# Linear attention and a gated MLP in one order: the first half of the written order is new, and the f, k and q loads span 112 rows

## The chip, the cores and the metric

The kernel runs on one core of a Trainium2 chip. The metric is the device time of one execution in microseconds (us).

## What is computed

For 4 batches, 8 heads, 768 tokens and 48 channels a head, a linear attention with a decaying state; its output, 4 x 768 x 384, goes through a gated MLP with a spatial product over tokens.

```python
f = 1 / (1 + exp(-f_logit))
for t in range(768):
    state = f[t, :, None] * state + outer(k[t], v[t])     # per batch and head, 48 x 48
    y[t] = q[t] @ state
h = maximum(x @ w_in, 0)                                  # x: y of all heads, 384 wide; h: 1024 wide
u, v = h[..., :512], h[..., 512:]
v_n = (v - mean(v)) / sqrt(var(v) + 1e-6)
v_s = einsum('ts,bsd->btd', w_spatial, v_n) + b_spatial[:, None]
out = (u * v_s) @ w_out
```

## The kernel before

The attention goes in 24 chunks n of 128 tokens, six for each batch. Two heads share the 128 partitions: the channels of one on rows 0 to 47, of the other on rows 64 to 111. Rows 48 to 63 and 112 to 127 of the host array `fkq` are padding.

The whole program is one list, `PLAN`: each word is a step, a letter name and its numbers, and the steps are issued in the order of the list. Every engine, and the queue of SyncE (SP) that issues all loads, so works through its own part of the list strictly in that order; a step that waits holds up all that stand behind it on its engine. `BESIDES` names the steps that go to GpSimd (POOL) instead of their usual engine.

The steps of a chunk n:

- `LF:n` loads f, into row block 0 of one of three tiles `fkq`. For n below 6 (`SUMMED`) it loads 128 tokens x 384 from `fn` (192 KB), and `LK:n` loads k and q apart (512 KB). From 6 on, `LF:n` loads f, k and q in one (768 KB). `LQ:n` loads v (192 KB) into one of two tiles.
- `c:n` clamps f (L322), `e:n` takes exp and ln of it on ScalarE (ACT; L326, L327). `z:n` makes running sums: for n below 6 on TensorE (PE) by a product with a triangle (L337), later as a scan on VectorE (DVE; L332). `h:n` and `g:n` exponentiate the sums (ACT; L343, L348), `k:n` and `q:n` multiply them into k and q (DVE; L354, L358).
- `X:n` makes the products of q and k (PE, L382), `m:n` masks them (DVE, L392), `w:n` copies another part (ACT, L388). `YS:n` (L434), `kv:n` (L406) and `Yq:n` (L446) are products for the output and the state; `r0`, `r1`, `r2` (DVE; L412 to L425) carry the state on; `ys:n`, `xt:n`, `xh:n`, `xl:n` copy, transpose and split the output. `fm:n` notes the last decay of the chunk (POOL).

The MLP's weights come in six pieces of 768 KB (`LV`, `LU`, `LO`, L243) and go through `ca`, `ct`, `ch`, `cl` to a high and a low part. V and U pieces share two buffers `words`: a buffer is free when `ch` and `cl` of its piece are through, and the next of these loads waits for that. `w_spatial` comes in pieces of 384 KB (`LW`, L284), split by `wh` (ACT or POOL) and `wl` (DVE, L294). `V:b,u` (L491), `U:b,th,c` (L576), `S:b,th,c` (L590) and `O:b,th,tt` (L621) are the MLP's products; `vr`, `bs`, `na`, `nb`, `nc`, `vn`, `vh`, `vl` normalize v, `sg`, `sm`, `sh`, `sl` gate. V and U of a batch's half need its three chunks; S needs all six vn of its batch.

`D:count` issues products of zeros (L674) into a bank that nothing reads. A load of f, k and q may go out only when the steps that read its tile's old content are through: `LF:6` after `X:3`, `LF:7` after `X:4`.

Of the kernel before, what the change touches and what calls it, by code (L numbers as in the profile page):

```python
# [825 lines left out]
```

## Time and profile before

| | |
|---|---|
| median of 3 runs | 356.96 us (356.3 to 357.31) |
| the profiled execution | 356.21 us |
| its span, first to last instruction | 354.4 us |
| mean granted clock of TensorE | 0.979 |
| busy: PE, weight loads (PEld) | 338.0 us (95%), 313.5 us (88%) |
| busy: DVE, ACT, POOL | 211.9 us (60%), 172.5 us (49%), 77.6 us (22%) |
| moved by DMA | 36.15 MB, mean 102 GB/s |

Busy is the time in which an instruction of the engine ran. Products are pipelined, so a busy TensorE isn't one at its peak. The granted clock is a share of full speed (2.4 GHz); 0.5 is 1.2 GHz. An average over the span says little here, since the first 60 us and the rest have different limits; the rows below are by stretch.

### The profile page before, as it was taken

The numbers are of one execution on the slowest core, as the hardware profiler recorded it, in microseconds if no ns is written. First come the engines' busy times: TensorE is split into PE (matmuls) and PEld (weight loads), VectorE is DVE, ScalarE is ACT, GpSimd is POOL, SyncE is SP. The second block draws the span as 40 slices with busy tenths as digits, with TensorE's granted clock in tenths as the row PEclk, the third lists the DMA queues.
The fourth block names the chain that finished last, engine by engine and source line by source line (L and its number), as shares of the span: only waits on it lengthen the run. The fifth ranks groups of instructions, "written<-read, shape, count | busy, mean of one in ns | idle before, by whom it ended". The sixth has DMA issues, their size and how long they took to land.

```text
span 354.4 us, 10435 instructions
## 1 busy us (share of the span) xinstructions
PE 338.0 (95%) x4565; PEld 313.5 (88%) x4565; DVE 211.9 (60%) x407; ACT 172.5 (49%) x355; POOL 77.6 (22%) x94
## 2 busy tenths in 40 slices
...
GB/s 229 288 264 332 276 193 212 35 191 64 162 190 127 93 130 49 107 143 74 39 138 0 158 1 92 91 24 2 44 46 2 2 44 3 22 68 0 0 68 77
DMA packets 14838, 36.15 MB, mean 102 GB/s; under 512 B 1472, under 2 KB 10048, under 8 KB 14784
## 3 DMA queue, kind: packets, MB, share of 16 engines
...
q14 instruction: 16, 0.13, 0.1%
HBM read 30.67 MB, written 4.72 MB: 100 GB/s over the span
## 4 chain that ended last, share of the span: by engine, by line
PE 84%; DVE 5%; DMA 5%; ACT 1%; SPq 1%; issue 1%; POOL 1%; DVEq 0%; ACTq 0%; POOLq 0%
PE mm L590 29%; PE mm L621 14%; PE mm L576 13%; PE mm L491 12%; PE bp L382 6%; DMA fkq<-fkq 5%; PE bp L434 3%; PE bp L446 3%; PE bp L406 2%; PE mm L458 2%; DVE q L358 1%; DVE fkq L354 1%; POOL fkq L322 1%; PE mm L337 1%; DVE w_spl L294 0%
## 5 line engine op out<-in xcount | busy, mean ns | idle before, releaser
L606 POOL TENSOR_TENSOR uT<-gt,uT 128x384 f32<-128x384 f32 x32 | 34.5, 1087 | 151.8 <-DVE gt L599 64.0
L599 DVE TENSOR_TENSOR gt<-mm,b_bc 128x384 f32<-128x384 f32 x32 | 17.7, 553 | 48.3 <-PE mm L590 48.2
L590 PE MATMUL mm<-w_sph,vnh 128*128 128x384 f32 x192 | 39.4, 340 | 0.0
L590 PE MATMUL mm<-w_sph,vnl 128*128 128x384 f32 x192 | 39.0, 338 | 0.0
L590 PE MATMUL mm<-w_spl,vnh 128*128 128x384 f32 x192 | 38.9, 338 | 0.0
L581 ACT ACTIVATE uT<-mm 128x384 f32<-128x384 f32 x32 | 15.5, 488 | 45.1 <-PE mm L576 41.1
L590 PEld LDWEIGHTS mm<-w_spl,vnh 128*128 128x128 f32 x192 | 34.2, 188 | 0.0
L590 PEld LDWEIGHTS mm<-w_sph,vnl 128*128 128x128 f32 x192 | 34.2, 188 | 0.0
L590 PEld LDWEIGHTS mm<-w_sph,vnh 128*128 128x128 f32 x192 | 33.8, 188 | 0.3
L322 POOL TENSOR_SCALAR fkq<-fkq 112x512 f32<-112x512 f32 (+1 forms) x14 | 23.7, 1692 | 45.6 <-DMA fkq<-fkq 26.4
L382 PE MATMUL bp<-q,fkq 48*64 48x112 f32 x768 | 24.8, 271 | 4.6 <-DVE q L358 4.1
L382 PEld LDWEIGHTS bp<-q,fkq 48*64 48x64 f32 x768 | 20.2, 141 | 6.6 <-DVE q L358 4.6
L614 DVE TENSOR_TENSOR gl<-uT,gh 128x384 fp32r<-128x384 f32 x32 | 17.5, 563 | 13.8 <-ACT gh L610 13.8
L610 ACT CAST gh<-uT 128x384 fp32r<-128x384 f32 x32 | 16.0, 511 | 19.6 <-POOL uT L606 18.8
L354 DVE SCALAR_TENSOR_TENSOR fkq<-fkq 112x512 f32<-112x512 f32 x24 | 17.8, 742 | 10.9 <-ACT fkq L348 5.6
L567 DVE TENSOR_TENSOR vnl<-vr,vnh 128x512 fp32r<-128x512 f32 x21 | 14.8, 716 | 15.6 <-ACT vnh L557 15.6
L332 DVE TENSOR_TENSOR_SCAN fkq<-runs,fkq 112x512 f32<-112x512 f32 x18 | 23.2, 1296 | 0.2 <-ACT fkq L327 0.2
L576 PE MATMUL mm<-xTh,w_inh 128*128 128x384 f32 x96 | 23.0, 348 | 0.0
L505 ACT ACTIVATE vr<-mm 128x512 f32<-128x512 f32 x24 | 14.3, 598 | 18.0 <-PE mm L491 17.6
L491 PE MATMUL mm<-w_inh,xTh 128*128 128x512 f32 x72 | 22.3, 417 | 0.0
L576 PE MATMUL mm<-xTh,w_inl 128*128 128x384 f32 x96 | 22.1, 338 | 0.0
L621 PE MATMUL mm<-w_outh,gh 128*128 128x384 f32 x96 | 22.1, 346 | 0.0
...
## 6 DMA issues: line engine op xcount, KB each, us to landing
fkq<-fkq SPq DMA_DIRECT2D x18, 768.0 KB, 5.2
val<-vv SPq DMA_DIRECT2D x24, 192.0 KB, 4.3
out<-osb SPq DMA_DIRECT2D x23, 192.0 KB, 2.0
words<-w_cv SPq DMA_DIRECT2D x4, 768.0 KB, 8.3
fkq<-fkq SPq DMA_DIRECT2D x6, 512.0 KB, 5.9
late<-w_cv SPq DMA_DIRECT2D x2, 768.0 KB, 5.7
fkq<-fn SPq DMA_DIRECT2D x6, 192.0 KB, 3.0
...
```

The source lines that it names most:

```text
L322: other("c", n, nc.vector).tensor_scalar(f, f, -LOGIT_MOST, None, op0=ALU.max)
L332: return nc.vector.tensor_tensor_scan(f[0:DP], runs, f[0:DP], 0.0, op0=ALU.mult, op1=ALU.add)
L354: other("k", n, nc.vector).scalar_tensor_tensor(k, f, 1.0 / F_LEAST, k, op0=ALU.min, op1=ALU.mult)
L382: nc.tensor.matmul(sc[to, e, cs], k[dr, at:at + C], qs[n % 2][dr, j, chunk], start=True, stop=True)
L491: nc.tensor.matmul(acc, xs[:, c, ut * P:(ut + 1) * P], ws[:, c, G:FF], start=i == 0, stop=i == 3 * KX - 1)
L576: nc.tensor.matmul(acc[:, 0:TH], ws[:, kx, cs], xs[:, kx, :], start=i == 0, stop=i == 3 * KX - 1)
L590: nc.tensor.matmul(acc[:, 0:TH], vns.of((b, ks))[va][:, cs], w_sp_s[wb][:, ks, th * TH:(th + 1) * TH], start=i == 0, stop=i == 3 * KS - 1,)
L599: nc.vector.tensor_tensor(gts.take((b, th, c)), mm.of(("s", b, th, c))[:, 0:TH], b_bc[:, th * TH:(th + 1) * TH], op=ALU.add)
L606: nc.gpsimd.tensor_tensor(uT, gts.of((b, th, c)), uT, op=ALU.mult)
L610: nc.scalar.copy(gs.take((b, th, c), HU)[0], uTs.of((b, th, c)))
L614: nc.vector.tensor_tensor(lo, uTs.of((b, th, c)), hi.bitcast(F32), op=ALU.subtract)
L621: nc.tensor.matmul(acc[:, 0:DM], gs.of((b, th, c))[ga][:, ts], w_out_s[wb][:, c, :], start=c == cs[0] == 0 and ga == wb == 0, stop=c == cs ...
```

## The change

Three things change.

1. The first half of `PLAN` is written anew, up to the step `xt:11`; from there to the end it is word for word the old one. Products of zeros: 11, 5 and 3 before (19), now 4, 5, 3 and 4 (16).
2. `BESIDES`, up to chunk 13: q:5, q:6, q:7, q:8, q:11, q:13, the casts wh:1,0 and wh:0,1, and vn:0,4, vn:0,5, vn:1,1, vn:1,2 now go to POOL, r2:1 and r2:4 too, c:4 and c:15 as well. c:3, c:5, c:6, c:7 and r2:0, r2:8, r2:12 go back to DVE.
3. The host array has 112 rows in place of 128 for each pair of heads, and the loads of f, k and q span 112 partitions: 672 KB in place of 768, 448 in place of 512. The compute steps read rows 0 to 111, as before.

```diff
-    constants LF:0 LF:1 units:1 W0 c:1 c:0 e:0 units:0 D:11 LF:2 c:2 e:1 z:0 LQ:1 LV:0 g:0 z:1 LK:0 h:0 k:0 q:0 LK:1 g:1
+    W0 LF:0 constants c:0 units:0 LF:1 c:1 e:0 LK:0 LK:1 D:4 e:1 z:0 LV:0 LQ:0 g:0 h:0 k:0 units:1 z:1 g:1 runs h:1 q:0
...
-    c:1 c:3 r2:0 c:5 r2:2 c:6 r2:3 c:7 c:9 c:8 r2:6 c:10 r2:7 r2:8 c:13 r2:10 r2:12 c:16 c:17 r2:14 c:19 r2:16 c:20
-    r2:18 c:22 r2:22
+    c:1 c:4 wh:1,0 r2:1 r2:2 r2:3 q:5 r2:4 wh:0,1 q:6 c:8 q:7 r2:6 c:9 q:8 vn:0,4 vn:0,5 c:10 r2:7 q:11 c:13 r2:10
+    vn:1,1 q:13 vn:1,2 c:15 c:16 c:17 r2:14 c:19 r2:16 c:20 r2:18 c:22 r2:22
...
-            nc.sync.dma_start(ins[n % 3], fkq[b, u])
+            nc.sync.dma_start(ins[n % 3][0:DP], fkq[b, u])
...
-        nc.sync.dma_start(ins[n % 3][:, 1:3], fkq[b, u, :, 1:3])
+        nc.sync.dma_start(ins[n % 3][0:DP, 1:3], fkq[b, u, :, 1:3])
...
-        y = np.full((B, NU, P, J * T), pad, np.float32)
+        y = np.full((B, NU, DP, J * T), pad, np.float32)
```

What the new list does to the queues shows in the order of each engine's instructions. A row names the line (all lines of the changed kernel are one higher), the operation, and the tile it writes and reads; the number behind a tile's name tells its buffers apart (`fkq_112`, `_113`, `_114` hold chunks 0, 1, 2, then 3, 4, 5).

The head of SP's queue before: LF:0 to LF:2, LQ:1, LV:0 (words_157), LK:0, LK:1, LQ:0, LV:1 (words_158), LF:3.

```order
L308 DMA fkq_112<-fn 128x384
L308 DMA fkq_113<-fn 128x384
L308 DMA fkq_114<-fn 128x384
L318 DMA val_116<-vv 128x384
L243 DMA words_157<-w_cv 128x2x768
L314 DMA fkq_112<-fkq 128x1024
L314 DMA fkq_113<-fkq 128x1024
L318 DMA val_115<-vv 128x384
L243 DMA words_158<-w_cv 128x2x768
L308 DMA fkq_112<-fn 128x384
```

And now: LF:0, LF:1, LK:0, LK:1, LV:0, LQ:0, LQ:1, LF:3, LF:2, LV:1.

```order
L309 DMA fkq_112<-fn 128x384
L309 DMA fkq_113<-fn 128x384
L315 DMA fkq_112<-fkq 112x1024
L315 DMA fkq_113<-fkq 112x1024
L244 DMA words_157<-w_cv 128x2x768
L319 DMA val_115<-vv 128x384
L319 DMA val_116<-vv 128x384
L309 DMA fkq_112<-fn 128x384
L309 DMA fkq_114<-fn 128x384
L244 DMA words_158<-w_cv 128x2x768
```

LK:0 has moved from the sixth place to the third, and LF:2 from the third to the ninth, behind LF:3, which needs k:0.

The same queue further on, before: LU:1 (words_157), LW:0,1, LQ:4, LF:6, LK:5, LU:0 (words_158), LF:7.

```order
L243 DMA words_157<-w_cv 128x2x768
L284 DMA late_161<-w_spT 128x2x384
L318 DMA val_115<-vv 128x384
L310 DMA fkq_112<-fkq 128x1536
L314 DMA fkq_114<-fkq 128x1024
L243 DMA words_158<-w_cv 128x2x768
L310 DMA fkq_113<-fkq 128x1536
```

And now: LU:1 (words_158), LQ:4, LU:0 (words_157), LF:6, LQ:5, LK:5, LW:0,1, LF:7.

```order
L244 DMA words_158<-w_cv 128x2x768
L319 DMA val_115<-vv 128x384
L244 DMA words_157<-w_cv 128x2x768
L311 DMA fkq_112<-fkq 112x1536
L319 DMA val_116<-vv 128x384
L315 DMA fkq_114<-fkq 112x1024
L285 DMA late_161<-w_spT 128x2x384
L311 DMA fkq_113<-fkq 112x1536
```

LU:0 now stands ahead of LF:6 and LK:5.

DVE's queue around the sixth chunk, before: k:5, z:6, q:5, xl:2, r0:4, r1:4, two wl, r2:4, m:5, cl:U,1, q:6; k:6 is next.

```order
L354 SCALAR_TENSOR_TENSOR fkq_114<-fkq_114 112x512
L332 SCALAR_TENSOR_TENSOR fkq_112<-runs,fkq_112 112x512
L358 TENSOR_TENSOR q_124<-fkq_114,F_122 112x8x64
L473 TENSOR_TENSOR xTl_137<-mm_131,xTh_136 128x3x128
L414 TENSOR_TENSOR sB_127<-bp_135,sA_125 112x192
L420 TENSOR_TENSOR sA_126<-bp_135,sB_127 112x192
L294 TENSOR_TENSOR w_spl<-spat_160,w_sph 128x2x384
L294 TENSOR_TENSOR w_spl<-late_161,w_sph 128x2x384
L425 TENSOR_TENSOR sA_126<-sA_126,F_121 112x192
L392 TENSOR_TENSOR sc_118<-bp_134,mask 128x512
L272 TENSOR_TENSOR w_inl<-words_157,w_inh 128x3x256
L358 TENSOR_TENSOR q_123<-fkq_112,F_121 112x8x64
```

And now: c:6, xl:2, ct:U,1 (three), r0:4, r1:4, k:5, z:6, c:7, wl:2,0, cl:U,1; m:5 and k:6 are next.

```order
L323 TENSOR_SCALAR fkq_112<-fkq_112 112x512
L474 TENSOR_TENSOR xTl_137<-mm_131,xTh_136 128x3x128
L258 TENSOR_SCALAR words_158<-words_158 128x768
L259 SCALAR_TENSOR_TENSOR words_158<-words_158 128x768
L260 SCALAR_TENSOR_TENSOR words_158<-words_158 128x768
L415 TENSOR_TENSOR sB_127<-bp_134,sA_125 112x192
L421 TENSOR_TENSOR sA_126<-bp_134,sB_127 112x192
L355 SCALAR_TENSOR_TENSOR fkq_114<-fkq_114 112x512
L333 SCALAR_TENSOR_TENSOR fkq_112<-runs,fkq_112 112x512
L323 TENSOR_SCALAR fkq_113<-fkq_113 112x512
L295 TENSOR_TENSOR w_spl<-spat_160,w_sph 128x2x384
L273 TENSOR_TENSOR w_inl<-words_158,w_inh 128x3x256
```

The q steps and r2:4 have left this queue, and c:6 and c:7, which wait for LF:6 and LF:7, have come into it.

## Rows read from the trace of the kernel before

**Rows 1.** Busy time by long stretches: the stretch and its length in us, busy us and count of each engine, the granted TensorE clock, the DMA engines' share and GB/s.

```profile
0.00:60.00 60.00, 51.17 (x1090) 41.64 (x1091) 46.64 (x82) 46.42 (x92) 19.59 (x29) 0.91 0.75 253
60.00:120.00 60.00, 60.00 (x1006) 55.86 (x1005) 51.65 (x97) 36.13 (x73) 13.75 (x18) 1.00 0.41 139
120.00:344.00 224.00, 223.88 (x2456) 213.39 (x2455) 113.14 (x229) 88.70 (x188) 44.30 (x47) 1.00 0.16 53
```

**Rows 2.** The same by stretches of 4 us, from 12 to 48; the engines stand in the order PE, PEld, DVE, ACT, POOL.

```profile
12.00:16.00 4.00, 3.56 (x80) 3.33 (x84) 3.24 (x6) 0.94 (x2) 0.63 (x1) 0.50 0.72 201
16.00:20.00 4.00, 4.00 (x126) 3.67 (x120) 3.90 (x8) 2.67 (x7) 1.56 (x3) 0.70 0.80 276
20.00:24.00 4.00, 3.06 (x86) 2.29 (x84) 3.50 (x7) 2.31 (x6) 0.19 (x1) 1.00 0.68 208
24.00:28.00 4.00, 3.63 (x51) 2.85 (x51) 3.59 (x6) 3.33 (x7) 0.00 (x0) 0.65 0.99 308
28.00:32.00 4.00, 3.66 (x146) 3.23 (x144) 2.94 (x7) 2.46 (x6) 2.69 (x4) 0.92 0.99 359
32.00:36.00 4.00, 3.52 (x85) 2.81 (x89) 3.84 (x7) 3.19 (x7) 1.15 (x1) 1.00 0.92 327
36.00:40.00 4.00, 4.00 (x76) 3.00 (x68) 3.59 (x5) 2.57 (x6) 2.78 (x3) 1.00 1.01 364
40.00:44.00 4.00, 3.25 (x133) 2.85 (x133) 3.97 (x7) 4.00 (x10) 1.20 (x1) 1.00 0.52 204
44.00:48.00 4.00, 3.63 (x76) 2.64 (x74) 4.00 (x7) 3.88 (x9) 2.80 (x2) 1.00 0.46 147
```

**Rows 3.** The chain of waits over the first 70 us: start, length in us, what. A DMA's length runs from its issue to its landing. L382 is X, L491 V, L576 U.

```profile
3.15 7.84 DMA fkq<-fkq
...
11.09 0.69 DVE fkq L354
...
12.44 3.27 PE bp L382 x64
...
17.78 4.88 DMA fkq<-fkq
...
23.36 0.35 DVE sA L425
...
24.37 1.04 PE bp L382 x32
...
30.19 5.98 DMA fkq<-fkq
...
47.36 0.61 DVE fkq L354
...
48.01 1.00 PE bp L382 x32
49.01 0.48 PE bp L446 x30
...
49.49 2.29 PE mm L491 x9
...
63.17 1.79 PE mm L576 x9
```

**Rows 4.** DMA issues of the page: out<-in, queue, count, KB each, median us from issue to landing.

```profile
fkq<-fkq SPq DMA_DIRECT2D x18, 768.0 KB, 5.2
val<-vv SPq DMA_DIRECT2D x24, 192.0 KB, 4.3
words<-w_cv SPq DMA_DIRECT2D x4, 768.0 KB, 8.3
fkq<-fkq SPq DMA_DIRECT2D x6, 512.0 KB, 5.9
fkq<-fn SPq DMA_DIRECT2D x6, 192.0 KB, 3.0
```

**Rows 5.** ACT in order of time: start us, us, line, operation, tiles. g:0 and h:0.

```profile
6.78 0.60 ACT L348 ACTIVATE fkq<-mm 112x512 f32<-112x512 f32 x1
7.27 0.59 ACT L343 ACTIVATE F<-mm 112x512 f32<-112x512 f32 x1
```

**Rows 6.** DVE in order of time, as above: the second cl:V, and r2:4. The last row is from the view of the tile fkq: the clamps on DVE with the least, median and greatest ns.

```profile
29.69 0.95 DVE L272 TENSOR_TENSOR w_inl<-words,w_inh 128x768 fp32r<-128x768 f32 x1
...
44.52 0.76 DVE L425 TENSOR_TENSOR sA<-sA,F 112x192 f32<-112x192 f32 x1
...
L322 DVE TENSOR_SCALAR fkq<-fkq x10: 353/416/828, 3.2 to 229.7; 112x512 f32<-112x512 f32 x7, 128x384 f32<-128x384 f32 x3
```

**Rows 7.** PE in order of time: the first and second group of zeros, and two products that came after a stop (idle us and its releaser in brackets).

```profile
2.11 2.53 PE L674 MATMUL mm<-junk 128*128 128x256 bf16 x11 [2.11 <-DVE rescale L212]
...
8.41 0.72 PE L674 MATMUL mm<-junk 128*128 128x256 bf16 x5
...
22.46 0.26 PE L446 MATMUL bp<-sA,q 48*64 48x48 f32 x2 [0.57 <-POOL ends L367]
...
24.37 1.04 PE L382 MATMUL bp<-q,fkq 48*64 48x112 f32 x32 [0.74 <-DVE q L358]
```

**Rows 8.** POOL: its two-input product by shape, from the groups by line (busy us and mean ns of one, then idle before), and its clamps from the view of the tile fkq.

```profile
L606 POOL TENSOR_TENSOR uT<-gt,uT 128x384 f32<-128x384 f32 x32 | 34.5, 1087 | 151.8 <-DVE gt L599 64.0 <-ACT uT L581 62.8 <-ACT fkq L348 20.7
...
L322 POOL TENSOR_SCALAR fkq<-fkq x14: 1163/1488/3148, 3.9 to 209.9; 112x512 f32<-112x512 f32 x11, 128x384 f32<-128x384 f32 x3
```

More of the change, by code (lines that the diff above doesn't have):

```diff
@@ new lines @@
+    e:13 r1:10 r2:10 LQ:12 LF:14 sh:0,0,2 na:1,0 nb:1,0 sg:0,1,3 sm:0,0,0 h:12 g:12 xt:9 S:0,1,1 sh:0,0,3 nc:1,0
+    sg:0,1,0 c:14 z:13 q:12 sl:0,0,3 ca:O,0 YS:11 ur:0,1,0 k:12 kv:11 ys:10 X:12 LF:15 r0:11 r1:11 Yq:11 vn:1,1 e:14
+    h:13 g:13 xt:10 xh:10 sg:0,1,1 z:14 LQ:13 xh:9 k:13 xl:9 ys:11 m:12 sm:0,1,3 fm:12 q:13 S:0,1,2 YS:12 w:12 xl:10
+    kv:12 X:13 sg:0,1,2 vh:1,1 r0:12 sh:0,0,0 Yq:12 U:0,1,2 vn:1,2 c:15 ct:O,0 r1:12 sh:0,1,3 w:13 LF:16 r2:12 xt:11
+    xh:11 xl:11 ys:12 sl:0,0,0 V:1,3 U:1,0,2 ur:0,1,2 vn:1,0 vh:1,0 vl:1,0 h:14 q:14 V:1,5 vl:1,1 m:13 sl:0,1,3 vr:1,5
@@ new lines @@
+    k:16 e:17 vh:1,5 q:16 z:17 sh:0,1,1 LF:18 V:2,1 w:15 YS:15 kv:15 X:16 ur:1,0,0 vr:2,1 w:16 xh:14 r0:15 bs:2,1 Yq:15
+    vl:1,5 xl:14 m:16 c:18 sl:0,1,0 sl:0,1,1 LQ:17 r1:15 fm:15 r2:15 U:1,0,1 ur:1,0,1 h:17 LF:19 ys:15 S:1,0,0 q:17 c:19
+    e:19 sg:1,0,0 S:1,0,2 S:1,1,1 od:0,0,2 g:17 V:2,2 k:17 sg:1,0,2 YS:16 kv:16 sm:1,0,2 od:0,0,1 r0:16 X:17 Yq:16
+    vr:2,2 LQ:18 r1:16 r2:16 sm:1,0,0 O:0,1,0 sg:1,1,1 fm:16 fm:17 ur:1,0,3 S:1,0,1 z:19 sg:1,0,1 sh:1,0,0 e:18 xt:15
+    z:18 bs:2,0 O:0,1,2 bs:2,2 m:17 h:18 S:1,1,2 sl:1,0,0 w:17 g:18 ys:16 q:18 oc:0,1,0 k:18 YS:17 kv:17 r0:17 X:18
@@ new lines @@
+    sg:2,0,1 ur:2,0,1 sm:2,0,1 S:2,0,3 xt:20 h:22 sl:1,1,0 w:21 U:2,0,2 oc:1,0,0 q:22 g:22 k:22 ur:2,0,2 sm:2,0,2 LQ:22
+    LQ:21 YS:21 sg:2,0,3 kv:21 sl:1,1,3 bs:3,1 r0:21 X:22 Yq:21 r1:21 O:1,1,2 S:2,1,0 U:2,1,3 od:1,0,2 sg:2,1,0 ur:2,1,3
+    r2:21 S:2,0,0 sg:2,0,0 sm:2,0,0 sh:2,0,2 S:2,1,3 sl:2,0,2 xh:20 xl:20 e:23 oc:1,1,2 z:23 O:1,1,0 h:23 g:23 V:3,2
+    sg:2,1,3 od:1,0,1 vr:3,2 bs:3,2 od:1,0,0 O:1,1,1 ys:21 xt:21 oc:1,1,1 U:2,0,3 ur:2,0,3 sm:2,0,3 sh:2,0,1 q:23
+    oc:1,1,0 na:3,0 nb:3,0 k:23 od:1,1,2 sm:2,1,3 S:2,1,2 S:2,1,1 LQ:23 sg:2,1,2 sh:2,0,3 nc:3,0 fm:22 fm:23 U:2,1,1
```

106 lines of the change are left out of this document (46 added, 60 removed).

## The prediction, made before the changed kernel ran

> **What bounds the kernel now.** I read busy time in long stretches first. TensorE is busy for 51.17 of the first 60 us, for all of the next 60, and for 223.88 of the 224 us after that [rows 1]. So from 60 us on the kernel goes at the rate of its products, and only the first 60 us have anything to give: 8.83 us without a product, and a mean granted clock of 0.91. The stretches of 4 us show that nearly all of this lies ahead of 48 us: VectorE (DVE) is busy for 32.57 of the 36 us from 12 to 48, the 16 DMA engines are near full from 24 to 40, and the granted clock is 0.50 to 0.70 from 12 to 20 and 0.65 from 24 to 28 [rows 2]. The chain of waits names what holds the early products [rows 3]: the first k and q of step X:0 land at 10.99 us (3.15 + 7.84), DVE's k:0 starts at 11.09 and X:0 at 12.44; LK:2 lands at 22.66 and X:2 starts at 24.37; LF:6 lands at 36.17, its clamp, exponent, running sum, k:6 and q:6 follow, and X:6 starts at 48.01. Loads decide, and behind each of them the DVE queue.
>
> **The mark.** X:6 is a good mark because both orders put the same products ahead of it: z:0 to z:5, X, YS and kv of chunks 0 to 5, Yq:0 to Yq:4, xt:0 to xt:4 and V:0,0 to V:0,2. Only the products of zeros differ (19, now 16). From step xt:11 on both lists are one. If TensorE stays full behind X:6, as it does before, the time moves by as much as X:6 does.
>
> **The start.** LK:0 had 1,536 KB in front of it in the SP queue, now 384 (sizes in [rows 4]). From LK:0 at 10.99 to LF:6 at 36.17 the queue brought 7,232 KB (the loads of its order by their sizes), 287 KB a us [rows 3, 4]. LK:0 with 448 KB of its own would be complete 1,216 KB sooner: 4.2 us, at 6.7. Then its factor is late next: g:0 ends at 7.38 and h:0 at 7.86 on ScalarE (ACT) [rows 5], and with units:1 moved behind h:0 nothing delays them. k:0 at about 7.5: **3.5 us earlier**.
>
> **Work on DVE between k:0 and k:6.** q:5 and q:6 go to GpSimd (POOL): 2 x 0.61. One half of the w_spatial remainders (L294) now stands behind k:6: 0.87. The state decays r2:1 (0.35) and r2:4 (0.76) go to POOL, r2:0 comes at the 0.35 of r2:1: 0.76 less. In come the clamps c:3, c:5 and c:2, which stood ahead of k:0 (0.36 each), and c:6, c:7 (0.42 each); c:4 leaves: 1.56 more [rows 6]. Sum: 1.22 + 0.87 + 0.76 - 1.56 = **1.3 us less**; I take 1.0, as the steps overlap a little. On ACT two weight casts of 0.8 us leave for POOL, which has slack (0.00 to 2.80 busy in 4 us) [rows 2].
>
> **New waits in the DVE queue.** Before, DVE stood 3.4 us of the 36 (36 - 32.57). With the work pulled forward it meets loads that aren't there. c:3 waits for LF:3, which SP may issue only after k:0 and which stands behind 2,432 KB: complete at 13.0 by the rate above, 1 to 1.5 us of wait. k:2 waits for LK:2, 4,224 KB in: 10.99 + (4,224 - 2,048)/287 = 18.6, about 1 us. The long one is c:6. DVE would reach it at about 33: it has 39 instructions from k:0 to there, at 32.57 us for the 60 from 12 to 48 [rows 2] 21.2 us, with 2.5 of waits so far and some 1.5 at the start for g:1 and X; LF:6 stands 9,248 KB in, at 36.1; and if the queue moves as in the full stretch from 24 to 40 (340 GB/s, the mean of its four rows [rows 2], 332 KB a us), at some 34.5, since LU:1 ahead of it can't go out before cl:V,1 has freed its buffer at about 27. That is 2 to 3 us with xl:2, ct:U,1, r0:4, r1:4, k:5 and z:6 queued behind. Together 4.0 to 6.0 us of waiting in place of 3.4: **0.6 to 2.6 us back**.
>
> **The sum.** k:6 ended at 47.97 [rows 3]. 47.97 - 3.5 - 1.0 + (0.6 to 2.6) = 44.1 to 46.1. X:6 then has YS:5 and kv:5 in front of it, which wait for m:5: 0.3 to 0.4 more, 44.4 to 46.5. Middle 45.4, **2.6 us ahead of 48.01**. The profiled execution took 356.21 us (span 354.4 and 1.8 around it), so it would take 353.6; it lies 0.75 below the median of the runs shown, 356.96, from which the forecast is **354.4 us**.
>
> **Edits costed at nothing.** The products of zeros take 0.14 to 0.23 us each (0.72/5, 2.53/11 [rows 7]) and lie where TensorE waits for loads; without that cover the 16 would cost 3 us. The 112-row loads are in the sizes above: 416 KB less up to LF:6, 1.45 us of it. On their price the trace has nothing, since every load in it spans 128 rows. The ends are a time that falls with the bytes (768 KB takes a median of 5.2 us to land, 512 KB 5.9 and 192 KB 3.0 to 4.3 [rows 4]: there the queue ahead hides the size) and a time that stays. I take the former, as full stretches move a steady number of bytes. The Trainium skill speaks against this edit: its page "SBUF — State Buffer", section "Door 1: The DMA port swizzle", says that a transfer is limited by the SBUF ports its partitions reach, and by its table rows 0 to 111 leave 12 ports with their full eight partitions and four with four, so the fullest port works as long as before. By that rule the 1.45 us fall away; by the bytes they stand; no run here shows which. On POOL the q of 112x512 has no row: the nearest is its two-input product of 128x384 at 1,087 ns, 1.45 us for 512 columns as an estimate, and the far end is the slowest clamp of 112x512 there, 3.15 us [rows 8]. q:5 and q:6 have 2 to 3 us before k:5 and k:6 are through, so I count them as hidden; at 3.15 us X:6 moves by about 1 us. Behind X:6 q:7, q:8, q:11, q:13 and four of the vn steps go to POOL too. The tightest is vn:0,4 and vn:0,5 ahead of S:0,0,1: two of 1.5 to 3.15 us on POOL, 3.0 to 6.3, with a small chain ahead and a cast and a subtraction behind, some 2 more. From k:8 on TensorE has X:8, Yq:7, U:0,1,3 and V:1,0, which is 1.00 + 0.48 + 1.79 + 2.29 = 5.6 us [rows 3], and YS and kv of two chunks besides. That covers it but for the far end, some 0.5 us.
>
> **Rivals.**
> *A load of 112 rows lasts as long as one of 128.* LF:6 lands 1.45 us later and c:6 with it: 2.6 - 1.45 = 1.15 us, 355.8 us. For it: time to landing hardly follows size. Against: bytes per us are steady where the queue is full. Chance 0.12.
> *The lower clock eats the gain.* Between X:4 and X:5 TensorE has some 8 us of products for 10 to 12 us, and all 16 products of zeros lie ahead of X:4. Two short stops of 0.57 and 0.74 us [rows 7] preceded the stretch at 0.65 and 0.92 [rows 2], in which 1.4 + 0.3 = 1.7 us were lost. One or two such falls behind X:5 give 1.7 to 3.4 back: -0.8 to 0.9 us, 356.1 to 357.8. For it: the gaps are new. Against: while TensorE waits for loads the level costs nothing. 0.18.
> *LU:0 holds up LF:6: slower.* In the new order LU:1 and LU:0 both stand ahead of LF:6, LQ:5 and LK:5 on SP, and each waits for a cl:V step on DVE to free its buffer; before, LF:6 and LK:5 went ahead of LU:0. Behind cl:V,0 come at most 2,400 KB up to LF:6 (8.4 us), then c:6, xl:2, ct:U,1, r0, r1, k:5, z:6, c:7, a wl, cl:U,1, m:5, k:6, 14 instructions, 8.3 us at 15.4 for the 26 from 32 to 48 [rows 2], 9 with the longer ct among them: X:6 some 18 us after cl:V,0. I have that end at 27.5. In the trace the second cl:V ends at 30.64 [rows 6], which would give 48.6; past 31.1 the kernel is slower by more than can be told, at 32 by 2 us: 359 us. For it: four waits for loads stand ahead of cl:V,0. Against: everything ahead of it starts 3.5 us sooner. 0.13.
> *More than that.* With the full rate throughout and c:6 unhindered X:6 comes near 43.5: 4.5 us, 352.5 us. 0.07.
> That the host array drops its rows and the loads shrink is plain from the order (112x1536 in place of 128x1536), so that the change doesn't happen isn't a rival.
>
> **How the numbers follow.** The forecast has 0.50 (353.4 to 355.5 by the ends of the sum). About 0.3% of the time, 1.07 us, is what a measurement of this kernel can tell from none. Faster by more: 0.50, 0.07 of the wider gain, 0.08 of the 112-row case and 0.04 of the clock: 0.69. Within: 0.04 and 0.11: 0.15. Slower: 0.13 and 0.03 of the clock: 0.16. The range leaves out the worst of the last and the best of the wider gain: 351.6 to 357.5.
>
> **What would show it.** Right: k:0 near 7.5, X:0 near 9, LK:2 landed by 18.6, DVE idle by 2 to 3 us in front of c:6, X:6 between 44.4 and 46.5, and TensorE full from there on. The 112-row loads: LF:6 near 35 with no more than 9.3 MB brought. Wrong: X:6 at 48 or later with cl:V,0 past 30 (the words buffers), a granted clock under 1 behind 42 us (the clock), a TensorE stop at the first S step behind 65 us (the vn steps moved to POOL), or a moved X:6 whose gain is gone by 120 us.

## The result, and the profile after

The change makes the kernel slower: 360.84 us median (359.19 to 365.61, four runs) beside 356.63 for the kernel before on the same chip (356.15 to 357.31), a ratio of 1.0117 with a 95% interval of 1.0076 to 1.0157. 354.4 had been forecast. Ratios leave disturbed executions out: 365.61 is one, order_128_wh_vn and start_c2_later below have one each, and so is the profiled one of stride128_load112, of which only the packets are read. The profiled execution took 359.19 us (span 357.5), 2.98 more than that of before. X:6, the mark, started at 50.01 us; 44.4 to 46.5 had been forecast, 48.01 was before. From X:6 to the end it is 307.5 us, before 306.4.

Long stretches of the changed kernel, columns as in [rows 1]:

```profile
0.00:60.00 60.00, 45.22 (x1035) 36.77 (x1036) 45.57 (x78) 44.46 (x87) 24.65 (x33) 0.97 0.80 232
60.00:120.00 60.00, 59.91 (x1043) 55.34 (x1041) 50.72 (x91) 37.12 (x74) 30.55 (x23) 1.00 0.45 125
120.00:344.00 224.00, 223.68 (x2454) 212.90 (x2454) 114.69 (x228) 88.99 (x189) 42.80 (x47) 1.00 0.18 53
```

TensorE is busy for 5.95 us less in the first 60, in part because its mean clock is higher (0.97 against 0.91) and because it got through fewer products there (1035 against 1090); later it is busy for as long as before. The DMA engines are busier (0.80 against 0.75) and move less (232 GB/s against 253). The same in stretches of 4 us, as in [rows 2]:

```profile
16.00:20.00 4.00, 2.76 (x111) 2.33 (x111) 2.85 (x8) 2.84 (x5) 1.26 (x2) 1.00 1.06 271
20.00:24.00 4.00, 2.04 (x64) 1.66 (x55) 3.86 (x5) 2.74 (x5) 3.14 (x3) 1.00 1.04 278
28.00:32.00 4.00, 2.38 (x111) 2.04 (x112) 3.43 (x7) 2.40 (x5) 0.72 (x1) 1.00 1.05 332
32.00:36.00 4.00, 2.14 (x34) 1.52 (x27) 3.05 (x7) 3.28 (x7) 0.51 (x1) 1.00 0.95 232
36.00:40.00 4.00, 4.00 (x50) 2.88 (x51) 2.64 (x4) 1.44 (x3) 0.00 (x0) 0.57 0.95 238
44.00:48.00 4.00, 4.00 (x100) 3.33 (x90) 4.00 (x7) 3.43 (x8) 4.00 (x3) 1.00 0.59 163
```

Read the last two columns: full engines move 232 to 278 GB/s in four of the first five rows, where shares of 0.92 to 1.01 gave 308 to 364 before [rows 2]; the rate depends on what is loaded, too (372 GB/s at 1.05 from 24 to 28, not shown). Read the first column too: TensorE stands for 3.48 of the 8 us from 28 to 36, where it stood for 0.82 before. The chain of waits (start, length, what; L492 is V, L447 Yq, L383 X) says on what:

```profile
27.58 0.33 PE mm L459 x3
27.91 0.25 PE bp L447 x5
28.16 1.61 issue
29.77 0.61 PE bp L447 x26
...
31.74 0.93 PE bp L383 x32
32.67 0.43 PE mm L492
33.09 1.86 issue
34.95 2.75 PE mm L492 x8
37.70 1.90 PE mm L338 x15
...
40.59 0.55 PE bp L447 x31
...
50.01 0.99 PE bp L383 x31
```

"issue" means that nothing in the profile releases the wait. Both stops stand inside a step: after 5 of the 31 products of Yq:2, and after the first of V:0,0. In the first 56 us the chain of the kernel before [rows 3] has no such row above 0.43 us. Behind them V:0,0 and z:5 run at a granted clock of 0.57, in part at the lower of the two levels, and kv:4 ends only at 40.6. From Yq:3's end GpSimd works without a gap up to X:6 (start, length, engine, line, tiles):

```profile
41.25 1.30 POOL L359 TENSOR_TENSOR q<-fkq,F 112x512 f32<-112x512 f32 x1 [6.74 <-PE bp L447]
42.49 0.65 POOL L368 COPY ends<-F 112x4 f32<-112x4 f32 x1
43.11 1.43 POOL L426 TENSOR_TENSOR sA<-sA,F 112x192 f32<-112x192 f32 x1
44.49 2.76 POOL L289 CAST w_sph<-late 128x768 fp32r<-128x768 f32 x1
47.20 1.53 POOL L368 COPY ends<-F 112x4 f32<-112x4 f32 x1
48.69 1.27 POOL L359 TENSOR_TENSOR q<-fkq,F 112x512 f32<-112x512 f32 x1
```

These are q:5, fm:4, r2:4, wh:0,1, fm:6 and q:6. On VectorE k:6 was done at 47.80, so q:6 comes 2.2 us after it. And the loads, as in [rows 4]:

```profile
fkq<-fkq SPq DMA_DIRECT2D x18, 672.0 KB, 5.3
...
fkq<-fkq SPq DMA_DIRECT2D x6, 448.0 KB, 7.0
```

The smaller loads land no sooner: 5.3 us against 5.2, 7.0 against 5.9.

VectorE from the start of k:0 to the end of k:6, columns as in [rows 1], first before (11.09 to 47.96), then now, and two of its steps in between (the wait of r0:4, and k:5):

```profile
11.09:47.96 36.87, 32.32 (x829) 26.65 (x829) 33.43 (x54) 25.65 (x51) 12.99 (x14) 0.86 0.79 270
7.34:47.80 40.46, 31.06 (x796) 24.93 (x796) 33.63 (x54) 28.54 (x55) 14.38 (x14) 0.96 0.89 261
```

```profile
40.73 0.36 DVE L415 TENSOR_TENSOR sB<-bp,sA 112x192 f32<-112x192 f32 x1 [1.95 <-PE bp L407]
...
41.47 1.63 DVE L355 SCALAR_TENSOR_TENSOR fkq<-fkq 112x512 f32<-112x512 f32 x1
```

VectorE starts 3.75 us sooner and ends 0.16 sooner: it works for as long (33.63 us against 33.43) and stands for 6.83 in place of 3.44.

### The profile page after: what moved, and what is told of

Its sections match the earlier page's. It is cut to its first block, busy times and chain, and to the rows that moved or that the text cites. A ratio compares the mean times of both kernels' runs of the same rounds, so it can differ in the third digit from the quotient of the medians.

```text
span 357.5 us, 10435 instructions
## 1 busy us (share of the span) xinstructions
PE 334.6 (94%) x4562; PEld 310.5 (87%) x4562; DVE 212.3 (59%) x400; ACT 172.4 (48%) x353; POOL 99.0 (28%) x103
## 3 DMA queue, kind: packets, MB, share of 16 engines
q1 hardware_dynamic: 14400, 33.23, 31.6%
## 4 chain that ended last, share of the span: by engine, by line
PE 87%; DMA 3%; ACT 2%; POOL 2%; DVE 2%; issue 2%; SPq 0%; POOLq 0%; ACTq 0%; DVEq 0%
PE mm L591 28%; PE mm L622 14%; PE mm L577 14%; PE mm L492 13%; PE bp L383 5%; PE bp L435 3%; PE bp L447 3%; DMA spat<-w_spT 2%; PE bp L407 2%; PE mm L459 2%; PE mm L338 1%; POOL sA L426 1%; DMA fkq<-fn 1%; POOL ends L368 1%; DVE fkq L355 1%
## 5 line engine op out<-in xcount | busy, mean ns | idle before, releaser
L607 POOL TENSOR_TENSOR uT<-gt,uT 128x384 f32<-128x384 f32 x32 | 35.3, 1111 | 138.0 <-ACT uT L582 62.8
L323 POOL TENSOR_SCALAR fkq<-fkq 112x512 f32<-112x512 f32 (+1 forms) x12 | 19.5, 1622 | 29.0 <-DMA fkq<-fkq 19.9
L383 PE MATMUL bp<-q,fkq 48*64 48x112 f32 x768 | 23.6, 261 | 3.0 <-POOL q L359 1.4
L355 DVE SCALAR_TENSOR_TENSOR fkq<-fkq 112x512 f32<-112x512 f32 x24 | 19.9, 828 | 9.6 <-ACT fkq L349 8.5
L492 PE MATMUL mm<-w_inh,xTh 128*128 128x512 f32 x72 | 22.5, 418 | 2.2 <-issue 1.9
L383 PEld LDWEIGHTS bp<-q,fkq 48*64 48x64 f32 x768 | 18.9, 134 | 5.7 <-DVE q L359 2.1
```

The costliest lines, as they stand in the source:

```text
L323: other("c", n, nc.vector).tensor_scalar(f, f, -LOGIT_MOST, None, op0=ALU.max)
L355: other("k", n, nc.vector).scalar_tensor_tensor(k, f, 1.0 / F_LEAST, k, op0=ALU.min, op1=ALU.mult)
L383: nc.tensor.matmul(sc[to, e, cs], k[dr, at:at + C], qs[n % 2][dr, j, chunk], start=True, stop=True)
L492: nc.tensor.matmul(acc, xs[:, c, ut * P:(ut + 1) * P], ws[:, c, G:FF], start=i == 0, stop=i == 3 * KX - 1)
L607: nc.gpsimd.tensor_tensor(uT, gts.of((b, th, c)), uT, op=ALU.mult)
```

## The experiments

Three theories were set up. **1, the rows:** a load of 112 partitions costs DMA time. **2, the instructions:** TensorE's own instructions come by DMA, and late while the engines are full. **3, GpSimd:** the work moved there sets X:6. X:6 and packet times below are from one profiled execution each; ratios are to the kernel before on the same chip, while the medians come from several chips.

One execution fixes X:6 only roughly. stride112_load128 below runs the instructions of the kernel before on other addresses and takes the same time (0.9988), yet its profiled execution (354.24 us) has X:6 at 45.93, where that of before (356.21 us) has 48.01. So a difference of X:6 of up to some 2 us between two kernels is not by itself the effect of the edit.

### The parts of the change apart

rows_alone is the kernel before with the row edit alone; order_128 is the change without it; pool_back is the change with most of GpSimd's new work taken back (the q and vn steps, wh:0,1 and r2:4; the clamps, r2:1 and wh:1,0 stay as in the change); order_128_pool_back is the change without the rows and with the same work taken back; engines_alone is the kernel before with the GpSimd table alone.

```diff
# rows_alone: kernel before          # order_128: the change, these three reversed
-  dma_start(ins[n % 3], fkq[b, u])
+  dma_start(ins[n % 3][0:DP], fkq[b, u])            (the same in step_LK)
-  y = np.full((B, NU, P, J * T), pad, np.float32)
+  y = np.full((B, NU, DP, J * T), pad, np.float32)
# pool_back: the change; order_128_pool_back: order_128 with the same edit
-  BESIDES = c:1 c:4 wh:1,0 r2:1 r2:2 r2:3 q:5 r2:4 wh:0,1 q:6 c:8 q:7 r2:6 c:9 q:8 vn:0,4 vn:0,5 ...
+  BESIDES = c:1 c:4 wh:1,0 r2:1 r2:2 r2:3 c:8 r2:6 c:9 c:10 r2:7 c:13 r2:10 c:15 ...
# engines_alone: kernel before with the whole BESIDES of the change
```

> The kernel before with only the loads of f, k and q cut to 112 partitions (host array without padding rows); order and engines as before. Theory 1 (a 112-partition load costs DMA time: the data packets of 4,096 bytes took a median of 253 ns in the changed kernel and 159 before): the packets are long here too, LF:6 lands no sooner than 36.2 us, X:6 at 48 to 49.5, 356.6 to 358.2 us. Theory 2 (the new order, not the rows, costs the time: TensorE runs out of instructions because loads stand back to back): packets about as before, time within 0.7 us of before. Prediction's own term (time by the bytes): LF:6 1.45 us sooner, up to 1.4 us faster.

> The changed kernel with loads of 128 partitions again (rows alone undone; order, zero products and engine choices stay). Theory 1 (the rows): packets of 4,096 bytes back near 160 ns, the two stops of TensorE that nothing releases (1.61 and 1.86 us at 28 and 33 us) go, X:6 at 47 or sooner, 355 to 357 us. Theory 2 (the order): the stops stay, 256 TensorE instructions apart, X:6 at 49 or later, 359 us or more. Theory 3 (GpSimd sets X:6): the stops may go, but q:6 on GpSimd still ends near 49, 358.5 to 360 us.

> The changed kernel with q:5 to q:8, q:11, q:13, wh:0,1, r2:4 and vn:0,4, 0,5, 1,1, 1,2 back on the engines they had before (VectorE and ScalarE); order and 112-row loads stay. Theory 3 (the GpSimd chain q:5, fm:4, r2:4, wh:0,1, fm:6, q:6 sets X:6 at 50.01 while k:6 ends at 47.80, and the vn steps cost about 1 us behind it): X:6 near 48, 357.5 to 358.7 us. Theories 1 and 2 (loads, instruction fetch): the stops at 28 and 33 us stay; the work only comes back to VectorE, which then is late instead: X:6 at 49 to 50.5, 359.5 to 361.5 us.

> The changed kernel with both undone: loads of 128 partitions, and the work that went to GpSimd back on VectorE and ScalarE. What is left of the change is the written order and its 16 products of zeros. Theory 2 (the order by itself costs): 358.5 us or more. Theories 1 and 3 (rows and GpSimd cost, the order gains what it set out to): X:6 at 45.5 to 47, 354.5 to 356 us, less than both kernels.

> The kernel before with the table of GpSimd's work of the changed kernel and nothing else: q:5 to q:8, q:11, q:13, wh:0,1, wh:1,0, r2:1, r2:3, r2:4 and four vn steps on GpSimd, the clamps c:3, c:5, c:6, c:7 on VectorE, c:4 and c:8 on GpSimd. In the new order these moves gained 2.7 us (360.1 to 357.4 without the row edit). Theory A (the moves relieve VectorE in any order): 353.5 to 355.5 us. Theory B (they pay only in the new order, which was written for them; in the old one the GpSimd chain r2:4, fm:6, q:6 and the vn steps come late): 356 to 359 us.

| Kernel | rows | order | GpSimd | median us | ratio, 95% interval | X:6, us |
|---|---|---|---|---|---|---|
| before | 128 | old | old | 355.97 | 1 | 48.01 |
| rows_alone | 112 | old | old | 359.96 | 1.0149 (1.0101 to 1.0198) | 49.76 |
| engines_alone | 128 | old | new | 367.82 | 1.0322 (1.0255 to 1.0390) | 56.06 |
| order_128_pool_back | 128 | new | mostly old | 360.10 | 1.0114 (1.0067 to 1.0161) | 52.01 |
| order_128 | 128 | new | new | 357.40 | 1.0053 (1.0024 to 1.0082) | 46.89 |
| pool_back | 112 | new | mostly old | 362.29 | 1.0202 (1.0165 to 1.0239) | 51.66 |
| the change | 112 | new | new | 360.84 | 1.0117 (1.0076 to 1.0157) | 50.01 |

The rows by themselves cost 1.0 to 2.0%, 3.6 to 7.0 us; theory 1 had expected up to about 2, so its sign stands and its size was too small. In the new order they cost 2.3 us with the new GpSimd work (1.0117/1.0053) and 3.1 with the old (1.0202/1.0114); by the intervals either figure may be 2 us off. With 128 rows X:6 is sooner by 1.1 us only, less than it differs between two executions of one order; the two stops stay and get shorter (1.34 and 1.31 us), and its time is above that of before: theory 1 had them gone, theory 2 had 359 us or more, and each has a part of it. Theory 3 has the wrong sign: with GpSimd's work taken back both kernels are slower, pool_back by more than any theory had. In order_128_pool_back the chain is short, but DVE, which works in order, then has q:5 at the head of its queue (VectorE's waits, 30 to 45 us: total, times, longest):

```profile
DVE q L359 <- PE bp L447: 5.7, 1, 5.7
```

q:5 must wait there until Yq:3 has read the buffer, and Yq:3 stands behind a TensorE stop of 2.96 us. In the old order the table of the change is far worse than either theory had (359 us at most): the clamps of f that it puts on VectorE (L322) block the queue there while their loads are on the way (the same view of engines_alone, 8 to 60 us):

```profile
DVE fkq L354 <- DMA fkq<-fkq: 6.0, 2, 5.3
DVE fkq L322 <- DMA fkq<-fkq: 5.0, 1, 5.0
DVE fkq L322 <- DMA fkq<-fn: 2.5, 1, 2.5
```

So order and table belong together, and only the rows can be judged alone. In rows_alone the queue stays full longer and brings less (columns as in [rows 2], where 36 to 40 had 364 GB/s and 40 to 44 a share of 0.52):

```profile
32.00:36.00 4.00, 3.64 (x87) 3.07 (x88) 3.74 (x8) 3.17 (x7) 1.29 (x1) 1.00 1.04 290
36.00:40.00 4.00, 3.51 (x73) 2.45 (x72) 3.21 (x5) 2.09 (x4) 0.97 (x1) 1.00 1.02 258
40.00:44.00 4.00, 3.06 (x73) 2.21 (x72) 2.81 (x4) 3.41 (x7) 1.14 (x3) 1.00 1.03 249
```

LF:6 landed at 38.88 there and at 36.17 before, with 416 KB less in the queue up to it.

### Why 112 rows cost

```diff
# stride128_load112: kernel before, host array of 128 rows
+  dma_start(ins[n % 3][0:DP], fkq[b, u, 0:DP])
# stride112_load128: host array of 112 rows, flat, 16 rows of zeros at the end
+  at = (b * NU + u) * DP;  dma_start(ins[n % 3], fkq[at:at + P])
# split64: kernel before
+  for at in (slice(0, C), slice(C, P)):  dma_start(ins[n % 3][at], fkq[b, u, at])
```

(the same in step_LK each time)

> The kernel before, its host array of 128 rows a chunk left as it is, but the loads of f, k and q take only rows 0 to 111 into partitions 0 to 111. It parts the two halves of the row edit. If the price comes from writing 112 partitions (112 packets for 16 DMA engines, seven each, so that they no longer stand on eight partitions each): packets of 4,096 bytes at a median of 220 to 260 ns as in the run with the rows alone (228.5), 358.5 to 361 us. If it comes from where the rows lie in the device's memory (a chunk of 672 KB in place of 768 KB): packets at 159 ns, time within 1.5 us of before.

> The kernel before with the host array of 112 rows a chunk (16 rows of zeros at its very end), but loads of 128 rows: each takes the first 16 rows of the next chunk into the partitions that nothing reads. The counterpart of the other. If the 112 partitions cost: packets at 159 ns, time within 1 us of before. If the place in memory costs: packets of 220 to 260 ns and 358.5 us or more.

> The kernel before with each 128-row load of f, k and q issued as two loads of 64 rows (partitions 0 to 63, then 64 to 127); bytes and packets stay 128 a load of 4,096 or 6,144 bytes. It asks why 112 rows cost. Theory S (a load is shared out evenly over the 16 DMA engines in order of its rows, so 128 rows put each engine on eight partitions of its own, and with 7 or 4 rows each neighbouring engines write to the same eight): the packets get longer here too, a median over 200 ns in place of 159, 357.5 us or more. Theory N (only the number 112 matters, as the load no longer fills the queues evenly): packets at 159 ns, and at most 1 us for the six more issues on SyncE at the start.

| Kernel | 4,096 B packets, median ns | 6,144 B, first 45 us | data moved, share of 16 engines' span | ratio, 95% interval |
|---|---|---|---|---|
| before | 159 | 234 | 35.40 MB, 29.8% | 1 |
| the change | 253 | 376 | 33.23 MB, 31.6% | 1.0117 (1.0076 to 1.0157) |
| rows_alone | 228.5 | 374 | 33.23 MB, 31.7% | 1.0149 (1.0101 to 1.0198) |
| stride128_load112 | 240 | 380 | 33.23 MB, 31.4% | 1.0114 (1.0028 to 1.0200) |
| stride112_load128 | 159 | 234 | 35.40 MB, 29.4% | 0.9988 (0.9953 to 1.0023) |
| split64 | 273 | 306 | 35.40 MB, 36.3% | 1.0317 (1.0248 to 1.0385) |

Where the rows lie in memory doesn't matter, the 112 partitions do. One packet carries one partition's row, and it takes about half as long again when the load spans 112 partitions. Two loads of 64 do the same with not a byte changed and cost 3.2%, 367.75 us: what theory S forecast came. The 3.2% also hold 24 more loads to issue, which no run takes apart from the packets. That neighbouring engines then write to the same partitions is the reason that theory S was built on; the trace doesn't show which engine wrote where, so that reason stays argued.

The Trainium skill, page "SBUF — State Buffer", section "Door 1: The DMA port swizzle", holds that a transfer runs at the rate of the ports its partitions reach, and that 64 partitions reach half of them; its section "Can I just issue two DMAs to hit both halves?" says that two transfers for the two halves don't add up. The runs agree for 64 rows (packets of 273 ns in place of 159, 1.0317). For 112 rows the prediction read no gain and no loss from the rule; measured is a loss of 1.0 to 2.0%.

### What stops TensorE

The trace records TensorE's instruction loads as packets of 16 KB, 38 of them in a queue of their own. Counting TensorE's records (weight loads, matmuls, a few waits) in order of start, the stops without a releaser stand at numbers 705, 961 and 1217: each is 256 behind the last, and 193 beyond a multiple of 256. A packet starts after TensorE has entered the block of 256 ahead of it:

| Kernel | enters a block | packet | reaches its end | goes on |
|---|---|---|---|---|
| before | 24.90 | 27.45 to 28.38 | 29.87 | 29.95 |
| before | 29.95 | 31.18 to 32.57 | 35.88 | 35.89 |
| the change | 17.25 | 21.03 to 22.34 | 21.98 | 23.62 |
| the change | 23.62 | 27.15 to 28.22 | 27.94 | 29.77 |
| the change | 29.77 | 32.30 to 33.56 | 32.60 | 34.95 |
| order_128 | 22.85 | 26.27 to 27.19 | 27.16 | 28.72 |
| order_128 | 28.72 | 30.92 to 31.93 | 31.54 | 33.35 |

Where it had stopped, TensorE goes on 1.3 to 1.6 us after the packet's end. In the rows of the new order the packet starts 2.2 to 3.8 us after the block is entered, and a block takes 4.6 to 6.4 us; the small products at the full clock run through one in 2.8 to 4.7. Before, the packets start 2.6 and 1.2 us after and are in time. That full DMA engines make the packets late is argued from this: the 1.2 us fell into a stretch with a share of 0.99, and no run takes the other loads away. The stop at 705, at 22 us, is put down to ScalarE by the profile, but lies at a block's end too.

The Trainium skill, page "Runtime: NRT & Kernel Launch", section "Instruction fetch mechanics", has the block of 256 instructions and 16 KiB, and calls the crossing mostly hidden. The size agrees with the trace; at the stops of the table the crossing isn't hidden: 1.3 to 1.9 us each.

To test it, the blocks were moved against the steps, with step E, tiny products of zeros (nc.tensor.matmul(mm.of("warm")[:, 0:16], junk[:, 0:P], junk[:, 0:16])), put where TensorE waits:

```diff
# order_128_shift: order_128
-  LK:1 D:4 e:1 ...  kv:0 r0:0 z:3
+  LK:1 D:4 E:32 e:1 ...  kv:0 E:32 r0:0 z:3
# order_128_nozero: order_128; after_nozero: the change with the same edit
-  X:2 D:5 xh:0 ...  wl:1,0 D:3 ys:1 ...  wh:2,0 D:4 w:3
+  X:2 xh:0 ...  wl:1,0 ys:1 ...  wh:2,0 w:3
# order_128_nozero_e12: order_128_nozero
-  LK:1 D:4 e:1
+  LK:1 D:4 E:12 e:1
```

> The changed kernel with 128-row loads and with 64 tiny products of zeros (16 columns) more on TensorE, 32 ahead of e:1 and 32 behind kv:0, both where TensorE waits. They move every later product 128 instructions down (a product is a weight load and a matmul). Theory 2 (TensorE's instructions come in blocks of 256, each fetched only after TensorE has entered the block before it, and late while the DMA engines are full): the stops that nothing releases again lie at instruction 193 of a block, 961 and 1217 by the new count, so 64 products sooner in the program than without the 64 (not in Yq:2 and V:0,0 any more), 1 to 2 us each; time 356 to 359 us. Rival (the stops belong to these steps, to what they read): they stay in Yq:2 and V:0,0 at the new counts 1089 and 1345.

> The changed kernel with 128-row loads, without the 12 products of zeros that stand inside the stream (D:5, D:3 and the second D:4; the four at the start stay). They are 24 of TensorE's instructions, about 1.6 us of work at full clock. The prediction's term (they cost nothing, TensorE waits there anyway): within 0.5 us of 357.4. If they hold the clock up: a stretch at half clock appears ahead of 45 us and the time is 1 us or more longer. If they help to starve TensorE of instructions (they move the blocks of 256 by 24): the stops move by 12 products, time 0.5 us or more less.

> The changed kernel with 128-row loads and without the 12 zero products inside the stream, but with 12 tiny ones (16 columns) at the start, where TensorE waits. So the blocks of 256 instructions lie from Yq:2 on where they lie with the 12 zero products in place. If the blocks make the stops: TensorE stops again at instructions 961 and 1217, in Yq:2 and V:0,0 (1 to 3 us together), X:6 at 46.5 to 48, 357.4 us or more. If the zero products made the difference: no such stop, X:6 at 45.6 as without the 12, 356.5 to 357.5 us.

> The changed kernel, with its 112-row loads, without the 12 zero products inside the stream. With 128 rows their removal moved the blocks by 24 instructions, and the stops at 961 and 1217 were gone (X:6 45.62 in place of 46.89). If the stops carry over: X:6 1 to 2 us sooner than 50.01, 358.5 to 360 us against 360.8. If the fuller DMA queues of the 112-row loads starve TensorE at any block: stops elsewhere, 360 to 362 us.

The chain of waits of order_128, then TensorE in order of time in order_128_shift (L407 is kv), then the chain of order_128_nozero_e12:

```profile
27.13 0.25 PE bp L447 x5
27.38 1.34 issue
28.72 0.61 PE bp L447 x26
...
31.61 0.43 PE mm L492
32.04 1.31 issue
33.35 2.13 PE mm L492 x8
```

```profile
23.64 0.36 PE L407 MATMUL bp<-val,W 64*48 64x48 f32 x16
25.89 0.40 PE L407 MATMUL bp<-val,W 64*48 64x48 f32 x16 [1.89 <-issue]
```

```profile
21.16 1.60 issue
...
26.71 0.25 PE bp L447 x5
26.96 1.66 issue
28.62 0.61 PE bp L447 x26
...
31.52 0.43 PE mm L492
31.94 1.58 issue
```

With 64 products put in, the stops leave Yq:2 and V:0,0; one of 1.89 us stands in the middle of kv:2, at number 961 by the new count; the one forecast for 1217 did not come. With 12 zero products taken out no stop above 0.5 us is left at a block's end (X:6 at 45.62), and with 12 tiny ones at the start they are back at 705, 961 and 1217, the last two in Yq:2 and V:0,0 behind the same product as in order_128 (X:6 at 47.06). The place is settled: blocks, not steps. Whether a block's end becomes a stop is not: it depends on when the packet starts and on how fast the products before it run.

The price in time is not. order_128_shift took 357.66 us (1.0047; 1.0015 to 1.0078, X:6 at 47.45), order_128_nozero 357.39 (1.0024; 0.9994 to 1.0053), order_128_nozero_e12 357.41 (1.0038; 1.0002 to 1.0073): the 1.4 us between the two marks don't show in the medians. after_nozero took 359.12 (1.0063; 1.0036 to 1.0089, X:6 at 51.47 in a profiled execution of 361.25, the slowest of its ten): lower than the change, with intervals that overlap, and with stops of 0.7, 1.9 and 1.9 us still at three block ends, 449, 705 and 1473.

### GpSimd's chain, piece by piece

```diff
# order_128_wh: order_128              # order_128_wh_vn: and this
-  r2:4 wh:0,1 q:6                     -  q:8 vn:0,4 vn:0,5 c:10
+  r2:4 q:6                            +  q:8 c:10
```

> The changed kernel with 128-row loads and the weight cast wh:0,1 back on ScalarE; all else of its GpSimd work stays. With 128 rows GpSimd ran q:5, fm:4, r2:4, wh:0,1, fm:6, q:6 one behind the other from 38.13 to 46.84 us, 2.76 of it wh:0,1, and X:6 started at 46.89 while k:6 ended at 44.68. Theory 3 (that chain sets X:6): X:6 at 45.0 to 45.6 us, 355.5 to 356.3 us. Rival (ScalarE, which takes 0.8 us more, or TensorE's own instruction stops set it): X:6 still at 46.5 or later, 357 to 358 us.

> The same with vn:0,4 and vn:0,5 on VectorE again as well. From X:6 on the new order takes 0.8 us longer than the order before (307.2 against 306.4 in the profiled runs). If GpSimd's slow vn steps (4.46 us for the two in the changed kernel) cause that: 0.5 to 0.8 us less than the kernel with wh:0,1 alone. If they are hidden: within 0.4 us of it, or slower where VectorE then lacks the time.

359.42 us (1.0069; 1.0027 to 1.0111) and 358.50 (1.0055; 1.0019 to 1.0091): no time is gained from either, and the first is slower than its theory and its rival had. In the profiled execution of the first (360.28) the packet for 1217 started 4.70 us after its block was entered, the stop was 3.04 us, and the clock stood at its lower level from 34.1 to 37.5 us. X:6 came at 47.62 with the cast off GpSimd. How far it came behind the end of kv:4 says more (the chain of order_128, then that of order_128_wh):

```profile
37.11 0.36 PE bp L407 x32
...
46.89 1.00 PE bp L383 x32
```

```profile
34.02 3.68 PE mm L492 x8
...
39.33 0.40 PE bp L407 x32
```

9.4 us in order_128, in the change and in order_128_nozero_e12 (9.1 to 12.9 in the other kernels of the new order that have the cast on GpSimd), 7.9 in both kernels with the cast on ScalarE: GpSimd's chain does hold X:6 up, by some 1.5 us, as theory 3 has it. But the 1.5 us don't reach the end: X:7 comes 13.1 us behind X:6 in both, 11.2 in order_128, and in the first VectorE holds TensorE up twice on the way, by 0.58 and 1.15 us, where order_128 has no such wait. So X:6 can be moved forward without the time following it. What keeps VectorE late there was not taken apart.

### The start by itself

```diff
# start_alone: kernel before; start_behind_LF2: the same behind LF:2
-  LF:0 LF:1 units:1 ... z:1 LK:0 h:0 k:0 q:0 LK:1 g:1
+  LF:0 LF:1 LK:0 LK:1 units:1 ... z:1 h:0 k:0 q:0 g:1
# start_c2_later: start_alone
-  LF:2 c:2 e:1 ... X:0 m:0 e:2
+  LF:2 e:1 ... X:0 m:0 c:2 e:2
```

> The kernel before with LK:0 and LK:1 moved up to stand right behind LF:1 in the order, and nothing else: the prediction's step of the start by itself. k:0 should start at 7.5 to 8 us in place of 11.09 and X:0 near 9. If the start is worth its 3.5 us in this order too: X:6 at 45 to 46 and 353 to 354.5 us. If the later loads decide (LK:2 and LF:6 stand behind the same bytes as before): X:2 within 1 us of 24.37, X:6 within 0.7 us of 48.0, 355.5 to 357 us.

> The kernel before with LK:0 and LK:1 moved up, but behind LF:2, so that c:2 does not wait: nothing else changes. k:0 at 8 to 8.5 us, X:0 at 9.5. If the early start is worth its time: X:6 at 45 to 46.3, 353 to 354.5 us, faster than both kernels. If LK:2 and LF:6 (the same bytes ahead of them) decide: X:6 at 47 or later, 355 us or more.

> The kernel before with LK:0 and LK:1 moved up right behind LF:1 and the clamp c:2 moved on VectorE to behind m:0, in front of e:2. k:0 at 7.5, X:0 at 9. If the early start is worth its time: X:6 at 45 to 46.3, 353 to 354.5 us. If the later loads decide: X:6 at 47 or later, 355 us or more. TensorE's stops at instructions 449 (0.79 us) and 961 (1.29) may come back, as with LK:0 and LK:1 moved alone, and take up to 1 us of it.

355.07 us (0.9961; 0.9915 to 1.0008; X:0 at 10.94), 355.56 (0.9961; 0.9935 to 0.9987; X:0 at 10.74) and 354.70 (0.9942; 0.9916 to 0.9968; X:0 at 8.92). The last two beat the kernel before, by 0.1 to 0.7% and 0.3 to 0.8%. In the first k:0 started only at 9.60, since c:2 stood ahead of it and waited for LF:2, in the second at 9.39, since LK:0 landed only at 9.28. X:6 was at 47.26, 47.05 and 49.97, nearer to where the expectations had it if the later loads decide. But LK:2 landed at 20.60, 20.85 and 20.74, 1.8 to 2.1 us sooner than before, with the same bytes in front of it. X:2 followed to 22.31 and 23.30; in start_c2_later it comes at 23.94, 0.4 sooner than before, because VectorE stands in front of k:2 until kv:1 is through on TensorE:

```profile
21.19 0.36 DVE L414 TENSOR_TENSOR sB<-bp,sA 112x192 f32<-112x192 f32 x1 [1.80 <-PE bp L406]
```

Its profiled execution, 357.9, is one of its slowest (352.78 to 358.18), and there TensorE stood at numbers 961 (in Yq, L446) and 1217 (in X, L382); TensorE's waits, 8 to 60 us:

```profile
PE bp L382 <- issue: 1.9, 1, 1.9
PE bp L446 <- issue: 1.2, 1, 1.2
```

## Why the prediction was wrong

**The start held.** k:0 began at 7.34 (7.5 forecast), X:0 at 8.69 and X:2 at 19.40, 5.0 sooner than in [rows 3].

**The new waits for loads came,** and were shorter: 0.90 us at c:3 (1 to 1.5), 1.04 at k:2 (about 1; LK:2 landed at 17.91, 18.6 forecast), 0.95 at c:6 (2 to 3; LF:6 at 35.34, VectorE there at 34.4 in place of 33). The prediction's own figures for the three add up to 4.0 to 5.5 us of waiting, not to 6.0.

**The sum failed** in one assumption, written nowhere as a term: that TensorE follows VectorE at once. X:4 came 4.1 us sooner than before and X:5 1.3 later. Between them lie the stops of 1.86 us and, ahead, of 1.61, then V:0,0 and z:5 in 4.65 us, part of it at the lower clock (3.15 in order_128, whose clock stayed up); kv:4 is late, and r0:4, k:5, z:6 and k:6 with it. VectorE's queue was costed as if loads alone could hold it up: of its 6.83 us of standing the three loads are 2.89, and waits for TensorE 2.52, 2.12 of it for kv.

Term by term, in the profiled execution: 47.97 for k:6 before, less 3.75 at the start (3.5 forecast), plus 0.20 of work (1.0 less forecast), plus 3.39 of waits (0.6 to 2.6 forecast) is 47.81; X:6 comes 2.2 behind it (0.3 to 0.4 forecast), 50.01. The work term failed although the moves took off the 1.3 us that they were costed at: k:5 took 1.63 us beside q:5 on GpSimd, where 0.69 had been counted, and some weight steps grew too. With q:5 back on VectorE, in pool_back, k:5 takes 0.68.

**The 112-row loads were mis-sized, with the wrong sign.** "A time that falls with the bytes", 1.45 us to the good, was taken; alone the edit costs 3.6 to 7.0 us, in the new order some 2 to 3. The full stretches of [rows 2] did show a steady rate, but of 128-row loads only. The rival of a load that lasts as long as before had the better direction, and also stopped short: the range had been bounded at "no gain".

**q:5 and q:6 "hidden" on GpSimd failed in the trace.** q:6 ended 2.2 us after k:6; 1 us had been the far end. Left out were fm, r2:4 and a 2.76 us cast in the same queue. The cast alone held X:6 up by some 1.5 us in order_128. Yet moving the work back makes the kernel slower (1.0202 against 1.0117), so the loss isn't won back there.

**The rivals.** LU:0 did not decide: the second cl:V ended at 28.68, before 31.1. The lower clock came, 0.57 from 36 to 40, but behind the stops, not as their rival: it cost 1.5 us (4.65 less 3.15). The vn steps took 4.46 us on GpSimd, within 3.0 to 6.3, and TensorE has no stop at the first S step: covered, as costed; putting two back gained no time that the intervals show. The zero products cost nothing that shows either (357.39 without 12 of them, 357.40 with).

**Behind X:6** 1.1 us went that the mark did not count; 1.0 of it lies between X:6 and X:14, where TensorE is idle for 0.74 us, before for 0.12. The rest wasn't traced to a place.

Open is why order_128 is no faster than before. Its profiled execution (355.81, X:6 at 46.89) was the fastest of its eight runs, and what its median of 357.40 looks like inside is not recorded. If the 1.6 us between them lie ahead of X:6, an estimate from these two times, X:6 stands near 48.5 in a run at the median, no sooner than before. The mean granted clock is on record for each run: 0.992 to 0.995 in the three fastest, 0.985 to 0.991 in the other five, so the lower level is likely a part of it. That the instruction packets start late by different amounts from run to run (2.20 us in order_128, 3.80 in order_128_pool_back, 4.70 in order_128_wh, all for the same block) fits, but no run shows it to be the cause.
